# K and Q transposed as pairs of heads in four-byte elements, in a fused kernel of segment-recurrent attention and linear-memory attention

## The chip, the cores and the metric

One Trainium2 chip, one of its cores. The metric is the device time of one execution in microseconds. The engines are TensorE (PE in the profile, its weight loads PEld), VectorE (DVE), ScalarE (ACT), GpSimd (POOL) and SyncE (SP, which issues DMAs).

## What is computed

Two mixers read the same x of 2048 rows by 512, and a gate for each row blends them. A is recurrent: 64 segments of 32 rows, each with 8 memory rows in front that are the first 8 output rows of the segment before. So there are 40 tokens, 32 heads of 128, and each segment's projections can only start when the one before has ended. B is local attention in 4 blocks of 512 rows with 32 heads of 16 and a linear memory; it does not depend on A.

```python
def _A_ref(x, mem0, Wq, Wk, Wv, Wo, seg_len):
    ...
    for s in range(n_seg):                       # 64
        h = concatenate([mem, x[:, s*32:(s+1)*32]], axis=1)      # 40 x 512
        q, k, v = (einsum('btd,dhe->bhte', h, W) for W in (Wq, Wk, Wv))
        scores = where(mask, einsum('bhqe,bhke->bhqk', q, k) * scale, -1e9)
        o = einsum('bhqk,bhke->bhqe', softmax(scores), v)
        o = einsum('bhte,hed->btd', o, Wo)
        mem = o[:, :8]
        outs.append(o[:, 8:])
...
g = sigmoid((x * gate_w).sum(-1, keepdims=True))
return g * A_ref(x, ...) + (1 - g) * B_ref(x, ...)
```

## The kernel before, in words

All weights of A lie in SBUF. A segment is one call of `p_seg` (L1434). Its 40 tokens are split: 24 rows of x and the 8 memory rows (32 tokens, in `hT`) go through the loop; the last 8 rows of x ("the rest") depend on nothing and are projected ahead for four segments at once in `p_rest` (L1364), 16 groups, with V of the rest carried through DRAM.

For each segment and each half r of the heads (16 heads):

- `project` (L1462) calls `wproj` (L1401): 16 matmuls in four column groups of 32, so that the four quadrants of a PSUM bank hold heads by tokens. K, Q and V each come out as 128 by 512. Q of the second half is done in two pieces of 256 columns. `copy` (L998) moves each piece to SBUF as bf16, on ACT (L1002) or DVE (L1002 too; L1000 where DVE is prescribed).
- `ktr` (L1475) transposes the pieces of K and Q on DVE in blocks of 32 by 32 (L1482), from `st` into `KT` (128 by 32 heads by 32 tokens) and `QT` (128 by 32 heads by 40 tokens). 128 transposes of K with 512 elements, 64 of Q with 512, 128 of Q with 256. Q of the rest comes from `rem_q` by a copy on POOL (L1459); it was transposed in `p_rest` (L1398).
- `p_s` (L1486): a matmul writes the mask (H), then 16 matmuls take the scores of one head each (L1497: `KT` of a head stationary, 32 columns; `QT` of a head moving, 40 columns), and 4 take those of the rest's keys for four heads each (L1501: the rest's K stationary, with a step of four elements; 4 by 16 columns of `QT` moving). ACT takes the exponential (L1505).
- `p_u`: sums by a matmul with ones (L1520), their inverse by two ACT operations (L1524, L1526), and products (L1528 on DVE, L1530 on DVE or POOL). Then values (PV L1561, PW L1570), evicted into `OT`, and `wo` (L1290): 64 matmuls (L1310), a transpose of the sum in PSUM (L1328), two small swaps (L1331) and an addition (L1333) that write the next segment's memory rows.

Matmuls of one segment's chain leave TensorE free in places; V's projections, the rest's projections, the output of the rest (`p_orest`) and all of B's work (logits L1142, exponentials L1160 on ACT, masks L1166 on POOL, values L1183, its outputs L1197 to L1245) fill them.

The order of the work on each engine is written out: `ORDER` (L15) is a packed list of operation numbers for each of TensorE, ACT, DVE, POOL and SP, and every engine runs its list in order. `sequences` (L472) unpacks it; `schedule` (L263) replays it to choose PSUM banks, and `waits` (L488) finds the semaphore waits from what each operation reads and writes. An operation that may run on two engines (an eviction: ACT or DVE) runs on the one whose list holds it. The first matmul into a PSUM slot of the pool "F" also waits for what the slot's later operations need, such as a staging buffer `stg` whose output transfer must have left (L270).

The costs given to operations (`cost=`) only served to make the lists; the chip does not see them.

Of the kernel before, what the change touches and what calls it, by code (L numbers as in the profile page):

```python
# [11 lines left out]
F32 = mybir.dt.float32  # L12
# [3 lines left out]
    "c-nPY2S60p)1P;RJ-DNsVj;vXV6WKu+d;8w)EJE#>=<K-1rvLV9UE$FF?K~X=2KD8U`2^FmT1JD7!?aB?S#F3`_0=cTaMg$g}vE%Q-1TCdCwgsjjsc;P5N9f(|hpZr|IU**3HYeK"  # L16
    ">`ry-t^Loz|iHL3)@Ux2yrm(V!g0`!T8${!7FCT^n{@sg|YRb7uZbuGh=>Qxcj147H2>4)7GP%c7A~6vjF}&KIrR&d+9vf9&@BCfZ^bmkQE;X8^`AO<^vBIPtF8%gK|gyNHeUe+8"
    "*G9&xNp(c~Af)axJ+qd0E_$0lx!;r{Pbz7X1bI9=MOorp}za<l7<5N<W7>0QSdUUV2anHSa^I*HGml^tWAyB4dPbQCGF}g^szF)F!s{=riHggRQ*JH@N1DcfgNf(aG&$6*NzqUI4"
    "(sZ*B1+oXCg4`wGDHm7wPeeRB=qRme?VX5fK0)P@H<>;b3|kq=;kb+Jr-eL88B-UMa~+^Vkye>54)4Q^(edC=FoUF{hU$Hu&ov`dde+!wHAEYS=8xfYU#7yOIBzGN!gZOFq7N{U*"
    "zC1H3k$WQ((DM{c2-)s&z1LT+tx@?nS6MVx%YTSKUYlS{=Jp=l{0aUCvGZRcUrdSWn;W`iDj}qfD9MXw>P<+q4U3aSkbS3yOLmu(Thk$G!A;%xUhldx<;kj%@;<xw~e#IL#bFV*z"  # L20
    "ob2+?Lf%=xo)4Dw6PJzjf?cm?q3VUR9OAVPK(mX`f}prB6!=bBVao^a0y8R(*#N^Am6a8Dh0*xF@fNy=QJXv)AfPCZ)7$k+C!rC0Gv)z!IYrxlJvbcTAu$RiGyQMY*<PorPrfw^O"
    "gezet<E%uH2_VU%9_U~LFoOS2Q7l${{yi+E%mz8>(H#Gmoh8bL09WGb8%PMj<WW>`cYrv$8o`E<avLvff;z)t57=>Jq0*Cb>T!<3hBSf@(lq(0q#AKVyzR<c@{if?OWzNFJ=QXqf"
    "a8f^;#4M+v=g!LJ7MK@d`dS!g<U|iTU61xCm?+AS+FPWdIY7-Sv?oXEPac5E?c>4~dC=>;f1pd$^*!EdW1e3PzT08};GdVT1*pl)nwT{*aNedUnF=r9@BoQiV2?ZTYuMDMog24qK"
    "X&*Jt7Zg~Z60f{!*6$@c^DF&}=8TZG|sImI4jQ=weAz?nZ}LWzKfK|VSIu53o9{;UVOD*&yMq9tK0Kr|Cpj9>A=k7GC+ydPodT>$<y;ClTlXldOH9<H20sW@5t-2BU}@_ist&=cQ"
    "WO93kn+oA3RB)^VA582*ZE#Q31v(XL&&zh3h$7(C^F7N>)3ooU;fh=KH!OXJ2aV)uc{ycBs4Tt+;!CkN4SXNm9MpTLetDtAlHGE)c<yZph-4DG3vl9CxK9FTM+<>}R74w}qmkiZ`"
    "y<-ZrPvc<;{CZm=2<dUXZwN+w8{$jwxA9@mg8}~G-eJx8jMyNV`{76|OW5aoCGlPWF;xKCVJ?V~S={*u$K4tQCkeDkMOLx>xoKEiru|eqN&XnVey@J_0K-C;R472jj8u@V_6*^n-"
    "sdnwHhVOpaOVIojIV#LU__90O69PQ3<3r?-v|xUMy<EV(i!+#BXNq8tZM(AT{|P>LDdHq9(_ItvFip&UM75vlGXk$$8PcwINtw*-=_X=DluqemV<#iVeMqJd#z=%jLSvvwq(@@pD"
# [12 lines left out]
    "|HpjH%?t~IQWQwCrO&2@jMJo_GH!v<~hQNJ4+ikCo2JD8J1a&!FH<3z@&4}(&tak(ynpo6$3|esG-@=d;0$(}dH-DavHu$Bh9@k{C2)T=z&d_04<<7`+-UQ}++1G8R-DJ&%hQu9%"  # L40
    "1_AL+X?)1?@hkNfFCA}?M0AOtS$5Iedn9B!V@$yRR~W-$%rfCH`dxs3Ey+M<1b%NyEeBz;UW&lICW21#_WuSllij&F(G9Oz{B+oj@&Yheh5il*LUgK*&RFpUz1C;H!+3ka`tJ~Px"
    "&T_*g?%PCJ8)fAc1T7jabneO3VI2R(N@2NNz&g1)`p1<-qXrNndwV3mPEjL$@=witRe}Wm;^pXheMdJg)<0FozEDLJ8yeY35AZ01fxp`?9W1V)Za*IWS~RHP|R&JbQJV11o1X2fe"
    "M=-RxrA235)9-?b<-#ZdD6-U)Es|qO4?*-YWU^eLUEv{0LZ4RT)>hGy!J@QaR9BrB>jnnUW|nqM-0h8-18gr+ZkCSE81#$J5~dO>Is#4F~Ml8*3h}2sTr_i!Uk#BpzA=Unh(?HxJ"
    "fq$+uh!iB9fTA{WeiAv6rDy9hV|n!%m&&x7^89haAV6DIt_s5Qt~1kZ=kw8lOK=i-mmOf#Q;P^s6u5?idDd};cd9*diCtqC0MY>wMRu~FJ*jIIVc!;Nt8B`|RNy4doRZXDtR!pvF"
    "Lxl?hkZb)xu!R8xm0xwGJ%jWYYz0nuQ`->fqC2cB0O_WkAD!2lXK+6AXFK3bDtdru6)L641lg&l_|EL=ZMqJB^H^Yfu1;;|_;db@&z5VLKo%-YA$qU?wrgqG^&}Gql=E1gRRm(H^"
    ">8r-VQj<ROlUunR*#4?bROtQMl*{oIaLFRhkQ#NunvHuYH~_<ZpHzc+ab{*sjV{aduwvqc{LcvV-3L#*)1oIe3H@&Ey=t-FROSpR5Pht75*thQkp-0Nz5kz}W*4mRR}DS<Fn!))s"
    "Xu*kxQpaQ*lmje2Up?^1vM#oR1E~0(YVPK1L(+=m;J`A!j0)5zvJ0UCoMG++BStnB4+!CPf^4E-mtX%$m(?5`T~wjSRxq=N9RrNI&Gz6R{Ww0crBcYu1sHA<PEr80b+y_hr4i;T0"
    "U4!ya~6iaHpoOCgrX*_+Sp;vEyDf^j`}7@H%Y&Yu`+q{=Dzb-V1&_ccm$eOc`-_QD-2fGhxoJ)IMtov;T5EOjlkR$)})|aV)BHzq0~YbalrDU-*0<)cCW8SAn-6<q(p)&aYk4kU9"
    "s2cYiT?NfSDDJ)tAlqV1TsL7hh8b?d^BA?;71vx4N2F(?<{P2l(yy>H*EOF2p^zJozJ0k#?GDd^2s-P5nfDBP~)dIR3k{1WJgZDo!@7kJ9i**`ENYp#qk9O)4P|FY|`$0_ApSgCz"
    "?{0le?B&hDnw*OQGuWEmyc)1sP(ECZ7{f`YfdVc3t0fr=<S`Tw(9=KgM88S<<V~|Pp{)wwk?NbsE5@WaH=FLbmgVW9-z-rx|+qgp&6BxVhGr?VG%>3ZJ-&Q!(^B_L0TawQ)RR48w"  # L50
    "5wqZbX`goO?i~$qr1R(dDs;<9^@IDh(CFz2Jm&L6r=w{tBsXDCpVdF|I*$3nTZ(EtnY+025rF6?cOh5+RwX;e(r?%DV>jY9h>f!OwQtpQILg*P9hp`49Rtn&KHs$*g|@i@Y=Galu"
# [525 lines left out]
T_TP = 0.72  # L577
# [6 lines left out]
class Kernel:  # L584
# [849 lines left out]
    def p_seg(self, s):  # L1434
# [16 lines left out]
        def by_head(t):  # L1451
            return t.rearrange("p (l q) -> p l q", l=4)
# [179 lines left out]
```

## Time and profile before

| | us |
|---|---|
| three runs | 828.84, 830.23, 834.37 (median 830.23) |
| the profiled execution | 829.86 |
| its span, first to last instruction | 827.8 |
| TensorE busy | 798.0 |
| DVE busy | 680.0 |
| ACT busy | 555.1 |
| POOL busy | 262.0 |
| granted TensorE clock, mean | 0.998 |

In a group of the profile stand line, engine, operation, destination and sources by the program's names, shapes, count, busy microseconds, mean nanoseconds of one, and the engine's idle time in front of them with what ended it. In a row of waits stand who waited, for whom, microseconds in total, times, and the longest. In the chain of waits stand start, length and what. A busy TensorE is not TensorE at its peak, since matmuls overlap.

### The profile page before, as it was taken

The page shows a single profiled execution, that of the slowest core. Times are in us where ns is not written, and L with a number is a line of the kernel's source. Part 1 is how long each engine was busy: PE and PEld are TensorE (multiplying, and loading weights), DVE is VectorE, ACT ScalarE, POOL GpSimd, SP SyncE. Part 2 cuts the span into 40 slices and gives each one's busy share as a digit, 9 for nine tenths or more (in the row PEclk, how much of TensorE's full clock was granted, in tenths as well). Part 3 has the DMA queues.
Part 4 walks back from the last instruction along what each step waited for, and adds up shares of the span by engine and source line. Part 5 has one row for each costly group of instructions (what it writes and reads, how often), then busy time and mean ns, then how long its engine had stood idle before and what let it go on. Part 6 is the DMA issues. An engine that isn't in the chain of part 4 may idle for free.

```text
span 827.8 us, 51780 instructions
## 1 busy us (share of the span) xinstructions
PE 798.0 (96%) x23605; PEld 509.8 (62%) x23613; DVE 680.0 (82%) x1606; ACT 555.1 (67%) x1264; POOL 262.0 (32%) x573
## 2 busy tenths in 40 slices
PE   8899999999999899999998999999999999999987
PEld 4456676657666476666666566565766665656655
DVE  4779778898888689787887998898877788987887
ACT  3667666776667567767666666667667667776763
POOL 3552231333223322431422232323513323323440
PEclk9999999999999999999999999999999999999999
DMA  9973201121200311111011101110111110000001
GB/s 331 411 239 56 52 26 35 34 51 27 53 19 14 52 26 36 34 39 39 15 38 46 38 21 42 18 40 20 40 46 27 26 34 17 15 25 22 22 21 36
DMA packets 71696, 45.14 MB, mean 55 GB/s; under 512 B 50046, under 2 KB 69942, under 8 KB 69942
## 3 DMA queue, kind: packets, MB, share of 16 engines
q1 hardware_dynamic: 70422, 40.92, 17.4%
q8 instruction: 185, 3.03, 1.4%
q10 hardware_dynamic: 1056, 0.92, 0.4%
q14 instruction: 33, 0.27, 0.1%
HBM read 30.33 MB, written 8.87 MB: 47 GB/s over the span
## 4 chain that ended last, share of the span: by engine, by line
PE 80%; DVE 7%; DMA 4%; ACT 3%; issue 2%; POOL 2%; SPq 1%; DVEq 0%; POOLq 0%
PE pb L1412 44%; PE pb L1310 16%; PE pb L1025 6%; PE pb L1142 3%; PE pb L1183 2%; PE pb L1561 2%; PE pb L1497 2%; DMA st<-in_gate_w_dram 2%; PE pb L1520 2%; DMA out_dram<-stg 1%; PE pb L1027 1%; DVE KT_sb L1482 1%; DVE QT_sb L1482 1%; DVE V_sb L1002 1%; PE pb L1570 1%
## 5 line engine op out<-in xcount | busy, mean ns | idle before, releaser
L1002 ACT ACTIVATE st<-pb 128x512 bf16<-128x512 f32 (+2 forms) x294 | 142.3, 506 | 93.8 <-PE pb L1412 73.7
L1160 ACT ACTIVATE PTB<-pb 128x640 bf16<-128x640 f32 x240 | 158.9, 704 | 36.7 <-PE pb L1142 27.9
L1412 PE MATMUL pb<-Wv_sb,hT 128*32 128x512 bf16 x2048 | 154.3, 380 | 0.7 <-issue 0.7
L1412 PE MATMUL pb<-Wq_sb,hT 128*32 128x512 bf16 (+1 forms) x3072 | 139.7, 309 | 0.1
L1412 PE MATMUL pb<-Wk_sb,hT 128*32 128x512 bf16 x2048 | 134.4, 380 | 0.6 <-DVE hT L1333 0.4
L1310 PE MATMUL pb<-Wo_sb,OT_sb 128*32 128x256 bf16 x4096 | 131.9, 273 | 1.1 <-issue 0.5
L1166 POOL TENSOR_SCALAR_AFFINE_SELECT PTB<-PTB 128x512 bf16<-128x512 bf16 x120 | 78.0, 650 | 111.7 <-ACT PTB L1160 105.8
L1310 PEld LDWEIGHTS pb<-Wo_sb,OT_sb 128*32 128x32 bf16 x4096 | 101.5, 96 | 14.5 <-issue 2.0
L1412 PEld LDWEIGHTS pb<-Wq_sb,hT 128*32 128x32 bf16 x3072 | 83.4, 97 | 43.3 <-issue 2.4
L1530 POOL TENSOR_TENSOR PT_sb<-PT_sb,rc_sb 128x64 bf16<-128x64 bf16 x81 | 29.1, 359 | 237.5 <-ACT rc_sb L1526 226.4
L1482 DVE STREAM_TRANSPOSE KT_sb<-st 128x512 bf16<-128x512 bf16 x128 | 89.0, 696 | 12.0 <-ACT st L1002 10.5
L1482 DVE STREAM_TRANSPOSE QT_sb<-st 128x256 bf16<-128x256 bf16 (+1 forms) x192 | 93.8, 507 | 3.4 <-ACT st L1002 1.6
L1412 PEld LDWEIGHTS pb<-Wk_sb,hT 128*32 128x32 bf16 x2048 | 57.2, 97 | 43.2 <-issue 2.7
L1002 ACT ACTIVATE OT_sb<-pb 128x320 bf16<-128x320 f32 (+1 forms) x138 | 56.7, 425 | 36.6 <-PE pb L1570 35.6
L1002 DVE CAST OT_sb<-pb 128x320 bf16<-128x320 f32 (+1 forms) x122 | 57.7, 480 | 20.3 <-PE pb L1570 19.9
L1524 ACT ACTIVATE rc_sb<-pb 128x160 f32<-128x160 f32 x128 | 38.9, 304 | 44.5 <-PE pb L1520 38.4
L1002 DVE CAST V_sb<-pb 128x512 bf16<-128x512 f32 x89 | 60.5, 680 | 7.4 <-PE pb L1412 6.1
L1412 PEld LDWEIGHTS pb<-Wv_sb,hT 128*32 128x32 bf16 x2048 | 50.4, 97 | 19.7 <-issue 0.6
L1328 DVE STREAM_TRANSPOSE pb<-pb 128x256 f32<-128x256 f32 x63 | 29.2, 463 | 36.0 <-PE pb L1310 35.6
L1505 ACT ACTIVATE PT_sb<-pb 128x224 bf16<-128x224 f32 x128 | 45.4, 355 | 11.4 <-PE pb L1501 8.5
L1002 ACT ACTIVATE stg<-pb 128x512 bf16<-128x512 f32 (+1 forms) x70 | 39.9, 572 | 15.0 <-PE pb L1412 12.1
L1528 DVE TENSOR_TENSOR PT_sb<-PT_sb,rc_sb 128x160 bf16<-128x160 bf16 x128 | 44.0, 343 | 5.7 <-ACT rc_sb L1526 4.0
(200 smaller groups left out, 1460.4 us busy)
## 6 DMA issues: line engine op xcount, KB each, us to landing
Wv_sb<-in_A_Wv_dram SPq DMA_DIRECT2D x4, 1024.0 KB, 10.0
Wk_sb<-in_A_Wk_dram SPq DMA_DIRECT2D x4, 1024.0 KB, 20.3
Wq_sb<-in_A_Wq_dram SPq DMA_DIRECT2D x4, 1024.0 KB, 27.4
Wo_sb<-in_A_Wo_dram SPq DMA_DIRECT2D x4, 1024.0 KB, 20.9
rest_v<-stg SPq DMA_DIRECT2D x112, 32.0 KB
rem_v<-rest_v SPq DMA_DIRECT2D x28, 128.0 KB
a_rows<-ao SPq DMA_DIRECT2D x63, 32.0 KB
stg<-a_rows SPq DMA_DIRECT2D x15, 128.0 KB
```

The costliest lines, as they stand in the source:

```text
L1002: self.P.op(("act", "dve"), (lambda a: a.activation(dst, src(), ACT.Copy), lambda d: d.tensor_copy(dst, src())), reads=reads, writes=write ...
L1025: ins = pe.matmul(out[32 * c:32 * c + 32], lhsT[:, 32 * c:32 * c + 32], rhs, start=start, stop=stop, tile_position=(0, 32 * c), **kw)
L1160: P.op("act", (lambda dst=dst, src=src: lambda a: a.activation(dst, src(), ACT.Exp, scale=0.25))(), reads=[pair], writes=["%s%d_%d" % (nam ...
L1166: P.op("gp", (lambda pt=pt, ii=ii: (lambda g: g.affine_select(pt, pt, ([[0, len(ii)]] if len(ii) > 1 else []) + [[1, 128]], ALU.is_ge, 0.0 ...
L1310: ins = pe.matmul(pb[so.b][p0:p0 + 32, 0:256], tok(r, g, l), half(h, d, q), start=(r == 0 and g == 0 and l < 2), stop=(r == 1 and g == 3 a ...
L1328: P.op("dve", lambda d: d.transpose(pb[so.b][:, 256:512], pb[so.b][:, 0:256]), reads=[so], writes=[rt], name="turn%s" % name, cost=0.46, p ...
L1412: ins = pe.matmul(self.pb[sl.b][32 * g:32 * g + 32, 0:hi - lo], x[:, c, 0:32], cols, start=(c == 0), stop=(c == C - 1), tile_position=(0, ...
L1482: op("dve", (lambda dst=dst, src=src: lambda d: d.transpose(dst, src))(), reads=["st%d%s" % (i, tag)], writes=["%sT%d%s" % (kind, r, tag)] ...
L1505: op("act", lambda a: a.activation(PT[:, r, :], pb[rb.b][:, 0:224], ACT.Exp, scale=SCALE), reads=[rb], writes=["PT%d" % r, "PT%dr" % r], n ...
L1524: op("act", lambda a: a.activation(rc[:, r, :], pb[rb.b][:, 0:160], ACT.Ln), reads=[rb], writes=[rr], name="ln%d_%d" % (s, r), cost=t_act( ...
L1528: op("dve", lambda d: d.tensor_tensor(mine[r], mine[r], by_head(rc[:, r, :]), ALU.mult), reads=[rp, rr], writes=[rp], name="nrm%d_%d" % (s ...
L1530: op(("dve", "gp"), tuple((lambda e: e.tensor_tensor(rest[r], rest[r], late(rc[:, r, :]), ALU.mult)) for _ in range(2)), reads=[rp + "r", rr],
```

## The change

Five things:

1. `KT` and `QT` hold pairs of heads: for each pair and token, the two heads' values side by side. Sizes stay.
2. The evictions of K and Q (`project`) and of Q of the rest (`p_rest`) write pairs: `paired` gives a destination that is contiguous and a source that reads, for each token i of a pair b, the two heads 32 columns apart in PSUM.
3. The transposes of K, Q and the rest's Q see the bf16 pairs as one f32: 256 elements in place of 512, 128 in place of 256. K of the rest is evicted and transposed as before.
4. The scores read one head of a pair with a step of two elements, stationary and moving (`l % 2`), and the matmuls of the rest's keys read `QT` in the same way, head by head, so that their columns stay in the old order. POOL's copy of the rest's Q moves the same 256 elements, in pairs.
5. `ORDER` is a new list. SP's part of it is the same; TensorE, ACT, DVE and POOL have other sequences. Of the evictions and other operations that may run on two engines, 66 net leave ACT, DVE gets 75 net, POOL loses 9 net. A few planning costs are changed with it.

The core of the diff (the list left out):

```diff
-        self.KT = t("KT_sb", [128, H, 32])
-        self.QT = t("QT_sb", [128, H, L])
+        self.KT = t("KT_sb", [128, H // 2, 32, 2])
+        self.QT = t("QT_sb", [128, H // 2, L, 2])
...
+    @staticmethod
+    def paired(dst, src):
+        return dst.rearrange("p (b i e) -> p b i e", i=32, e=2), lambda: src().rearrange("p (b e i) -> p b i e", e=2, i=32)
...
-        self.copy(st[:, 0:512], lambda: pb[sl.b][:, 0:512], 512, [sl], [rs], "r%sev%d_%d" % (kind, j, r), prio, dve=not j)
+        to, fro = st[:, 0:512], lambda: pb[sl.b][:, 0:512]
+        if kind == "q":
+            to, fro = self.paired(to, fro)
+        self.copy(to, fro, 512, [sl], [rs], "r%sev%d_%d" % (kind, j, r), prio, dve=not j)
...
-        P.op("dve", lambda d: d.transpose(dst, st[:, :]), reads=[rs],
+        src = st[:, :]
+        if kind == "q":
+            dst, src = dst.bitcast(F32), src.bitcast(F32)
+        P.op("dve", lambda d: d.transpose(dst, src), reads=[rs],
...
-        Kr, Qr = (self.group(k, s // 4).rearrange("p (h k s) -> p s h k", h=H, s=4)[:, s % 4] for k in "kq")
+        Kr = self.group("k", s // 4).rearrange("p (h k s) -> p s h k", h=H, s=4)[:, s % 4]
+        Qr = self.group("q", s // 4).rearrange("p (b k s e) -> p s b k e", b=H // 2, s=4, e=2)[:, s % 4]
...
-        op("gp", lambda g: g.tensor_copy(QT[:, :, SEG:L], Qr), reads=[rQr], writes=["qTr"],
+        op("gp", lambda g: g.tensor_copy(QT[:, :, SEG:L, :], Qr), reads=[rQr], writes=["qTr"],
...
+                fro = (lambda rb=rb, n=hi - lo: lambda: pb[rb.b][:, 0:n])()
+                if kind != "v":
+                    dst, fro = self.paired(dst, fro)
...
-                tag, src, h0, h1 = "" if lo == 0 else "b", self.st[i][:, lo:hi], 16 * r + lo // 32, 16 * r + hi // 32
+                tag, src, b0, b1 = "" if lo == 0 else "b", self.st[i][:, lo:hi].bitcast(F32), 8 * r + lo // 64, 8 * r + hi // 64
                 if kind == "k":
-                    dst = KT[:, h0:h1, :].rearrange("p h t -> p (h t)")
+                    dst = KT[:, b0:b1, :, :].rearrange("p b t e -> p (b t e)").bitcast(F32)
                 else:
-                    dst, src = QT[:, h0:h1, 0:SEG], src.rearrange("p (h t) -> p h t", t=SEG)
+                    dst = QT[:, :, :, :].rearrange("p b t e -> p (b t e)").bitcast(F32).rearrange("p (b t) -> p b t", t=L)[:, b0:b1, 0:SEG]
+                    src = src.rearrange("p (b t) -> p b t", t=SEG)
...
-                        ins = pe.matmul(pb[rb.b][32 * g:32 * g + 32, 56 * l + 16:56 * l + 56], KT[:, 16 * r + 4 * g + l, :], QT[:, 16 * r + 4 * g + l, :],
+                        ins = pe.matmul(pb[rb.b][32 * g:32 * g + 32, 56 * l + 16:56 * l + 56], KT[:, 8 * r + 2 * g + l // 2, :, l % 2], QT[:, 8 * r + 2 * g + l // 2, :, l % 2],
...
-                    ins = pe.matmul(by_head(pb[rb.b][32 * g:32 * g + 32, 0:224])[:, :, 0:16], Kr[:, h0:h0 + 4].rearrange("p h k -> p (h k)"), QT[:, h0:h0 + 4, 24:40],
+                    ins = pe.matmul(by_head(pb[rb.b][32 * g:32 * g + 32, 0:224])[:, :, 0:16].rearrange("p (b e) q -> p b e q", e=2),
+                                    Kr[:, h0:h0 + 4].rearrange("p h k -> p (h k)"), QT[:, b0:b0 + 2, 24:40, :].rearrange("p b t e -> p b e t"),
```

More of the change, by code (lines that the diff above doesn't have):

```diff
@@ L20 @@
[L20 to L27, printed above, removed]
@@ new lines @@
+    "o}-UlLQEyp%Znl@BL;{n;K2$&H>mTz4SFmT->}>Uj3k}Ax1#@|F)jy%a)CuJat}R+mVI0VSn<{jtTiAHr)-JHnVW?7+7^4Mjwxk0EEq7O){4P{F=1({YSvLVSQH!nLG4W_PiTg50"
+    "2~?Cjevt%qpGqX9JTf2%N|n43{DSW=?CJH`$aW^l;(b7AT27at_>WV<G2E+e=NC_xT4})(%_O;1cK|@!%sMuR5FrosV`z$GZL-ngj8W-QHDeyQR&AmT>-AJX~r9w&EP<vf>k13>}"
+    "YuMGWGzU!~8%&JQ-1f(c4LLI~N5IeQV0#?OF2!QE<RZ?L2efGsfP4iSf(uCn}cIN$12`{P+6F9gn+{LDZu1y+Cn%`e0KXaOQp5~=dwr?T)a2rjn0i#RdRP*D_60^lgLUW?-3T5AD"
+    "jybi^^oj}%>U%zo>Jb8OZ<N}L1(=#JDDoS_`pkgh2B0%=U>r|~rbo`cqusO2TW~0a<WCe1=<RUh>xlYGAT@awnt*sMpDAF5er(SIgaCr*VEC!Gp!1GiZ{)5^AJm?7j_+?@1XVC66"
@@ L80 @@
+    "otJL@)wL)-4c5)Eh!1`hDh{$_A@<Vb|sQd)O1)$wQuoV;zaLpB2sUUG%@u)ir8Hvb%k@Q&+V{k_rZ)KoSV_7cgq@(S1DUvNK#LR{$nJCG1bu4xjj1#%~6r$Iq{M$pvdwnLH^THot"
+    "upoOFI4qnez@%WfFs`viutmZQdpIeqVhij8t2925ks5$_xUQH^<o9B@t;c^s`Rkbk6PF+<V06afwJJsk~0Y%s!0(11U#Po^{Crh@eUSOyA{~o~Y!o_aVu1^h;qS`Oa0n|1KhDk~~"
+    "HKvKt?22LT~j&J#_d&CQ;15DVx(()emyhe-)x)ft#V(jKEIrad-db{{MseY1svyrY!5cK-+N&y_s"
 )
@@ L677, in alloc @@
             self.xT[1][:, :, :].rearrange("p c x -> p (c x)")[:, 0:1280], self.OT[:, :, :, :].rearrange("p g h q -> p (g h q)")]
-        self.spread = self.KT[:, 0:16, :].rearrange("p h t -> p (h t)").rearrange("p (l m) -> p l m", l=4)
+        self.spread = self.KT[:, 0:8, :, :].rearrange("p b t e -> p (b t e)").rearrange("p (l m) -> p l m", l=4)
         self.gwr, self.mem0 = self.st[1], self.st[0]
@@ L1327, in wo @@
             turned = lambda: pb[so.b][:, 256:512].rearrange("p (c e t) -> p e c t", c=4, e=2)
-            P.op("dve", lambda d: d.transpose(pb[so.b][:, 256:512], pb[so.b][:, 0:256]), reads=[so], writes=[rt], name="turn%s" % name, cost=0.46, prio=prio)
+            P.op("dve", lambda d: d.transpose(pb[so.b][:, 256:512], pb[so.b][:, 0:256]), reads=[so], writes=[rt], name="turn%s" % name, cost=0.468, prio=prio)
             for e in range(2):
@@ L1331, in wo @@
                 P.op(("act", "dve"), ((lambda a, dst=dst, src=src: a.activation(dst, src(), ACT.Copy)), (lambda d, dst=dst, src=src: d.tensor_copy(dst, src()))),
-                     reads=[so, rt], writes=["other%d" % e], name="swap%s_%d" % (name, e), cost=(0.24, 0.19), prio=prio)
+                     reads=[so, rt], writes=["other%d" % e], name="swap%s_%d" % (name, e), cost=(0.2, 0.195), prio=prio)
             P.op("dve", lambda d: d.tensor_tensor(mem[0], turned()[:, 0, :, 24:32], self.other[:, :, :], ALU.add),
@@ L1397, in p_rest @@
         dst = self.group(kind, j)[:, 512 * r:512 * r + 512]
-        P.op("dve", lambda d: d.transpose(dst, st[:, :]), reads=[rs],
-             writes=["rem%s%d" % (kind, j % 2)], name="r%stp%d_%d" % (kind, j, r), cost=T_TP, prio=prio)
+        src = st[:, :]
+        if kind == "q":
+            dst, src = dst.bitcast(F32), src.bitcast(F32)
+        P.op("dve", lambda d: d.transpose(dst, src), reads=[rs],
+             writes=["rem%s%d" % (kind, j % 2)], name="r%stp%d_%d" % (kind, j, r), cost=0.44 if kind == "q" else T_TP, prio=prio)
     def wproj(self, sl, kind, r, x, reads, name, prio, n, chunks=False, lo=0, hi=512):
@@ L1470, in project @@
                 dst, rd = (Vs[:, r, :], "V%d" % r) if kind == "v" else (self.st[i][:, lo:hi], "st%d%s" % (i, tag))
-                self.copy(dst, (lambda rb=rb, n=hi - lo: lambda: pb[rb.b][:, 0:n])(), hi - lo, [rb], [rd] + (["st%db" % i] if whole and kind != "v" else []),
+                fro = (lambda rb=rb, n=hi - lo: lambda: pb[rb.b][:, 0:n])()
+                if kind != "v":
+                    dst, fro = self.paired(dst, fro)
+                self.copy(dst, fro, hi - lo, [rb], [rd] + (["st%db" % i] if whole and kind != "v" else []),
                           "%sev%d_%d%s" % (kind, s, r, tag), prio)
```

117 lines of the change are left out of this document (59 added, 58 removed).

## The prediction

> **What bounds the kernel now.** I read the page's busy table first, then the stretches (busy time of each engine by window), the waits of TensorE, the chain of waits around the longest hole, and the groups by form for prices.
>
> ```profile
> span 827.8 us, 51780 instructions
> PE 798.0 (96%) x23605; PEld 509.8 (62%) x23613; DVE 680.0 (82%) x1606; ACT 555.1 (67%) x1264; POOL 262.0 (32%) x573
> ...
> 60.00:780.00 720.00, 702.95 (x21407) 457.20 (x21406) 604.68 (x1428) 495.62 (x1134) 220.09 (x467) 1.00 0.14 33
> 270.00:300.00 30.00, 26.66 (x743) 17.34 (x746) 20.64 (x46) 16.69 (x39) 8.36 (x18) 0.94 0.26 45
> 780.00:828.00 48.00, 40.27 (x1240) 25.93 (x1232) 36.86 (x85) 24.84 (x64) 12.60 (x28) 1.00 0.10 29
> ```
>
> In the stretches the first number is the length, the second TensorE's busy time, then PEld, DVE, ACT, POOL, then the granted clock. TensorE is busy for 798.0 of 827.8 us. Between 60 and 780 us it idles 720 - 702.95 = 17.05 us, and 30 - 26.66 = 3.34 us of that lie in one window, where the granted clock also falls to 0.94. Over the last 48 us it idles 7.7 us. The kernel is bound by TensorE's work, and the change removes none of it: all that can be won is what TensorE waits. What it waits for:
>
> ```profile
> PE pb L1412 <- DMA out_dram<-stg: 3.0, 3, 2.4
> PE pb L1142 <- ACT V_sb L1002: 2.2, 4, 0.6
> PE pb L1561 <- DVE PT_sb L1528: 1.4, 3, 1.0
> PE pb L1142 <- ACT stg L1002: 0.9, 2, 0.5
> PE pb L1142 <- DVE V_sb L1002: 0.8, 1, 0.8
> PE pb L1497 <- DVE QT_sb L1482: 0.7, 2, 0.4
> ...
> PEld pb L1497 <- DVE QT_sb L1482: 6.4, 24, 0.6
> PEld pb L1497 <- DVE KT_sb L1482: 1.8, 9, 0.3
> ```
>
> The transposes that the change shortens (L1482) end only 0.7 us of TensorE's idle time by themselves; the weight loads of the scores wait 6.4 + 1.8 = 8.2 us for them in 33 times, mostly while older matmuls still run. The other waits are for evictions and normalisations that stand in the queues of DVE and ACT. The one long hole is a transfer's:
>
> ```profile
> 278.90 0.10 SPq L986
> 279.01 0.04 issue
> 279.05 4.22 DMA out_dram<-stg
> 283.27 0.04 issue
> 283.32 1.89 PE pb L1412 x13
> ```
>
> An output transfer holds a staging buffer for 4.22 us, and TensorE stands behind it.
>
> **The transposes.** A transpose of 512 bf16 becomes one of 256 four-byte elements, one of 256 becomes 128.
>
> ```profile
> L1482 DVE STREAM_TRANSPOSE KT_sb<-st 128x512 bf16<-128x512 bf16 x128 | 89.0, 696 | 12.0 <-ACT st L1002 10.5
> L1482 DVE STREAM_TRANSPOSE QT_sb<-st 128x256 bf16<-128x256 bf16 x128 | 50.1, 412 | 0.7
> L1482 DVE STREAM_TRANSPOSE QT_sb<-st 128x512 bf16<-128x512 bf16 x64 | 44.6, 697 | 2.7 <-ACT st L1002 1.6
> L1328 DVE STREAM_TRANSPOSE pb<-pb 128x256 f32<-128x256 f32 x63 | 29.2, 463 | 36.0 <-PE pb L1310 35.6
> L1219 DVE STREAM_TRANSPOSE t_sb<-pb 128x512 f32<-128x512 f32 x32 | 22.5, 703 | 3.0 <-PE pb L1183 3.0
> L1398 DVE STREAM_TRANSPOSE rem_q<-stg 128x512 bf16<-128x512 bf16 x32 | 22.4, 701 | 1.9 <-ACT stg L1002 0.7 <-POOL QT_sb L1459 0.7
> ...
> L939 DVE STREAM_TRANSPOSE adot<-pb 128x128 f32<-128x128 f32 x4 | 1.2, 296 | 0.0
> ```
>
> 512 f32 take 703 ns and 512 bf16 696 ns: the price goes by elements, not bytes. For 256 four-byte elements in SBUF the bounds are 412 ns (as many bf16) and 463 ns (f32 in PSUM); I take 440. For 128 the bounds are 296 ns (from PSUM) and 412 - (696 - 412)/2 = 270 ns; I take 285. K: 128 x (696 - 440) = 32.8 us; Q whole: 64 x 257 ns = 16.4; Q halves: 128 x 127 ns = 16.3; Q of the rest: 32 x 261 ns = 8.4. DVE sheds 73.9 us (69 to 79 by the bounds). V and the rest's K stay as they are.
>
> **The new order.** SP's queue is the same, entry by entry, so no DMA is moved past another. TensorE runs the same 2979 steps; changes between its tile modes go from 382 to 380, which I cost at nothing. What moves is evictions, from ACT to DVE. Their prices:
>
> ```profile
> L1002 ACT ACTIVATE st<-pb 128x512 bf16<-128x512 f32 x168 | 100.2, 599 | 69.1 <-PE pb L1412 66.7 <-PE pb L1025 1.4
> L1002 ACT ACTIVATE st<-pb 128x256 bf16<-128x256 f32 x103 | 38.4, 384 | 9.0 <-PE pb L1412 7.0 <-DVE ao L1341 1.0 <-PE pb L1025 0.7
> L1331 DVE COPY other_sb<-pb 64x32 f32<-64x32 f32 x99 | 18.7, 189 | 5.0 <-ACT other_sb L1331 1.8
> L1002 DVE COPY st<-pb 64x256 f32<-64x256 f32 x40 | 17.1, 428 | 1.2
> L1002 DVE CAST st<-pb 128x512 bf16<-128x512 f32 x24 | 16.4, 685 | 5.4 <-PE pb L1412 5.3
> L1002 DVE CAST st<-pb 128x256 bf16<-128x256 f32 x25 | 9.9, 397 | 0.1
> ```
>
> Counted in the two orders, DVE takes over 57 evictions of 512 (K 26, Q 16, the rest 12, B's 3; 57 x 685 ns = 39.0 us) and 32 of 256 (12.7 us), and four products each for adot and t1 from POOL (8 at about 0.44 us, 3.5 us); it gives back 17 partial sums (7.3 us) and 6 small swaps (1.1 us). That is +46.8 us, so DVE ends near 680.0 - 73.9 + 46.8 = 653 us. ACT loses 57 x 0.599 + 32 x 0.384 = 46.4 us and gets 17 x 0.38 + 6 x 0.19 = 7.6 back: near 516 us. Neither is the bound, so these sums are not gains; they shorten queues in which TensorE's banks and operands stand.
>
> **The paired eviction** reads PSUM with a step of 32 elements between the two of a pair. No row steps so in PSUM. Lower end: nothing extra. L1331 reads runs of 8 with jumps, 32 elements in 189 ns, and L1002 reads 256 contiguous ones in 428: 1.07 ns an element between them, and contiguous reads of 256 and 512 differ by (685 - 397)/256 = 1.13, so jumps cost nothing there. Upper end: rate halved, that is (599 - 384)/256 = 0.84 ns more an element on ACT, 0.43 us for 512. I take nothing, by the nearer row. [...]
>
> **The scores** (L1497, L1501) read K and Q with a step of two.
>
> ```profile
> L1497 PEld LDWEIGHTS pb<-QT_sb,KT_sb x2048: 92/93/98, 50.4 to 818.5; 128*32 128x32 bf16 x187
> L1497 PE MATMUL pb<-QT_sb,KT_sb x2048: 179/179/193, 50.4 to 818.6; 128*32 128x40 bf16 x187
> L1501 PEld LDWEIGHTS pb<-QT_sb,rem_k x512: 105/107/113, 50.5 to 818.6; 128*32 128x32 bf16 x171
> L1412 PE MATMUL pb<-Wk_sb,hT 128*32 128x512 bf16 x2048 | 134.4, 380 | 0.6 <-DVE hT L1333 0.4
> L1412 PE MATMUL pb<-Wq_sb,hT 128*32 128x256 bf16 x2048 | 75.1, 274 | 0.0
> ```
>
> The one stepped weight load, L1501's with a step of four elements, takes 107 ns where the contiguous one takes 93 (medians). If step two costs the same, 2048 loads are 14 ns longer each, 28.7 us of PEld, which has 828 - 510 us to spare and runs beside matmuls: nothing on the path, and 28.7/4 = 7 us if that cover were gone, as four column groups load side by side. For the moving operand nothing is known. Lower end zero; upper end half rate: a column costs (380 - 274)/256 = 0.41 ns, each pair of heads' groups streams 4 x 40 columns in L1497 and 64 in L1501, 224 x 0.41 = 93 ns, in 128 steps 11.9 us, all on TensorE and so all on the path. I take zero, since even the stepped load at four elements lost only 14 ns over 32 columns, but with little confidence. [...]
>
> **POOL's copy** of the rest's Q (L1459) still moves 256 elements, read in runs of two now instead of single ones:
>
> ```profile
> L1459 POOL COPY QT_sb<-rem_q 128x256 bf16<-128x256 bf16 x64 | 28.1, 439 | 9.0 <-PE pb L1501 2.6 <-DVE rem_q L1398 1.6 <-PE pb L1570 0.4
> ```
>
> I leave it at 439 ns; POOL is idle two thirds of the time, and even 100 ns more would lie beside V's projections.
>
> **The sum.** Waits between 60 and 780 us without the transfer's window: 17.05 - 3.34 = 13.7 us. Bounds are none and all of it; I take half, 6.9 us, because half of what TensorE waits for stands in queues that get shorter and the rest is normalisation, POOL and issue. The last 48 us hold four segments with little other work; each has two transposes in series before its last scores, 257 + 127 ns shorter: 1.5 us. The transfer's hole stays, since SP's order does. The head, where weights arrive, stays. 829.9 us was the profiled execution's own time (span 827.8 and 2.1 around it), 0.4 below the median of 830.2. 829.9 - 8.4 + 0.4 = 821.9, forecast 822 us.
>
> **Rivals.** One: the stepped moving read runs at half rate. 822 + 11.9 = 834 us, within 1%; if nothing is gained either, 842. For it: the stepped weight load; against it: the load's loss is small. Two, the other side: the stepped PSUM read runs at half rate. ACT and DVE would still not be the bound, but each segment evicts five pieces before its scores, and TensorE's order is written for the old price; one eviction of 512 exposed in each segment is 64 x 0.43 = 27.5 us, 849 us. It decides from (838.5 - 822)/64 = 0.26 us exposed a segment on. Against it: L1331. [...] Three: DVE's relief is hidden. TensorE waited only 0.7 us for a transpose itself, and its other waits move elsewhere: 829 us. Four: nearly all waits go, the transfer's hole with them: 829.9 less 17.05 and half of the last 7.7 is 809 us.
>
> **How the numbers follow.** Forecast with reads free and about half the waits gone: 0.42, its own range 814 to 828. Four: 0.10. One: 0.22, of which 0.05 ends over 838.5. Three: 0.11. Two: 0.15. A measurement of this kernel tells about 1% from no change, 821.9 to 838.5 us. Faster: 0.10 + two thirds of 0.42, 0.38. Slower: 0.15 + 0.05 = 0.20. Within: 0.42. The range 810 to 840 leaves out rival two and the ends of one and four.
>
> **What would show it.** Right: transposes at 412 to 463 ns (256 f32) and 270 to 296 ns (128); evictions still at 599 and 685 ns; L1497's matmuls still at 0.18 us; DVE near 653 and ACT near 516 us busy; TensorE's busy time near 798 us and its idle time under 22 us. L1497's matmuls longer by 17 ns (40 columns) and busy time up by 12 us would show rival one; evictions of 512 at 0.8 us or more rival two. What would make the prediction wrong above all is TensorE's busy time itself changing.

## The result, and the profile after

The changed kernel took 824.47 us (median of 8 runs, 823.6 to 828.08) beside 830.87 for the kernel before: ratio 0.9928, interval 0.9904 to 0.9952. Measured again later it took 821.47 us, ratio 0.9880, 0.9858 to 0.9901. A ratio given here can differ by up to 0.0025 from the quotient of the two medians. The forecast was 822.0. So the size came out; which waits would go, and why, did not, as the experiments below show.

The profiled execution took 824.12 us. Its busy table, then its stretches (length, TensorE, PEld, DVE, ACT, POOL, granted clock):

```profile
span 822.2 us, 51771 instructions
PE 795.5 (97%) x23607; PEld 506.2 (62%) x23607; DVE 642.5 (78%) x1681; ACT 523.4 (64%) x1198; POOL 259.7 (32%) x564
```

```profile
60.00:780.00 720.00, 704.37 (x21549) 455.88 (x21545) 571.15 (x1494) 470.03 (x1084) 219.29 (x464) 1.00 0.14 33
270.00:300.00 30.00, 27.82 (x852) 18.99 (x841) 23.06 (x62) 16.52 (x40) 8.82 (x19) 1.00 0.17 39
```

TensorE's steady idle time fell only from 17.05 to 15.63 us, and 1.2 us of that lie in the window from 270 to 300. Its busy time fell by 2.5 us, with the same work. So in this execution idle time is not where most of the gain is seen. But a second execution of the same kernel, of 819.91 us, has a steady idle time of only 720 - 708.05 = 11.95 us:

```profile
60.00:780.00 720.00, 708.05 (x21655) 458.39 (x21658) 575.71 (x1510) 472.76 (x1090) 220.90 (x468) 1.00 0.14 33
```

Waits that the profile puts down to nothing ("issue") make 6.3 us of the idle time in the first execution, 2.8 in the second and 5.4 in before. Single executions of one kernel differ in idle time by more than the change that was to be read from it.

The prices, in groups by form:

```profile
L1002 ACT ACTIVATE st<-pb 128x512 bf16<-128x512 f32 x126 | 75.2, 598 | 71.0 <-PE pb L1422 69.6 <-PE pb L1029 0.5
L1497 DVE STREAM_TRANSPOSE KT_sb<-st 128x256 f32<-128x256 f32 x128 | 54.5, 426 | 7.0 <-ACT st L1002 5.5
L1002 DVE CAST st<-pb 128x512 bf16<-128x512 f32 x66 | 44.5, 674 | 9.6 <-PE pb L1422 8.9
L1497 DVE STREAM_TRANSPOSE QT_sb<-st 128x128 f32<-128x128 f32 x128 | 34.8, 285 | 2.7 <-ACT st L1002 2.0
L1497 DVE STREAM_TRANSPOSE QT_sb<-st 128x256 f32<-128x256 f32 x64 | 27.8, 434 | 5.1 <-ACT st L1002 3.8
L1002 ACT ACTIVATE st<-pb 128x256 bf16<-128x256 f32 x71 | 27.0, 384 | 16.1 <-PE pb L1422 11.1 <-DVE ao L1345 4.1 <-PE pb L1029 0.5
L1002 DVE CAST st<-pb 128x256 bf16<-128x256 f32 x57 | 22.9, 403 | 5.8 <-PE pb L1422 3.9 <-PE pb L1029 1.1
L1470 POOL COPY QT_sb<-rem_q 128x256 bf16<-128x256 bf16 x64 | 29.0, 453 | 43.5 <-PE pb L1516 35.9 <-DVE rem_q L1408 4.0
```

Transposes take 426 to 434 and 285 ns. Paired evictions take what the others took: 598 ns on ACT (599 before), 674 on DVE (685). The scores' reads (minimum, median, maximum in ns; L1512 was L1497, L1516 was L1501):

```profile
L1512 PEld LDWEIGHTS pb<-QT_sb,KT_sb x2048: 92/94/103, 49.3 to 812.5; 128*32 128x32 bf16 x187
L1512 PE MATMUL pb<-QT_sb,KT_sb x2048: 179/181/198, 49.4 to 812.5; 128*32 128x40 bf16 x187
L1516 PEld LDWEIGHTS pb<-QT_sb,rem_k x512: 105/108/116, 49.5 to 812.5; 128*32 128x32 bf16 x171
```

The step of two costs 1 ns in the load and 2 ns in the matmul. And the waits of the scores for the transposes (total us, times, longest), which were 6.4, 1.8 and (for `QT`) 0.7 us before:

```profile
PEld pb L1512 <- DVE QT_sb L1497: 2.4, 9, 0.4
PEld pb L1512 <- DVE KT_sb L1497: 1.7, 6, 0.4
...
PE pb L1512 <- DVE KT_sb L1497: 0.5, 2, 0.3
```

### The profile page after: what moved, and what is told of

It is laid out like the page before. It is cut to its first block, busy times and chain, and to the rows that moved or that the text cites. A ratio compares the mean times of both kernels' runs of the same rounds, so it can differ in the third digit from the quotient of the medians.

```text
span 822.2 us, 51771 instructions
## 1 busy us (share of the span) xinstructions
PE 795.5 (97%) x23607; PEld 506.2 (62%) x23607; DVE 642.5 (78%) x1681; ACT 523.4 (64%) x1198; POOL 259.7 (32%) x564
## 4 chain that ended last, share of the span: by engine, by line
PE 84%; DVE 7%; ACT 3%; DMA 2%; issue 2%; POOL 0%; SPq 0%; DVEq 0%; POOLq 0%
PE pb L1422 45%; PE pb L1314 17%; PE pb L1029 6%; PE pb L1146 4%; PE pb L1577 2%; PE pb L1187 2%; PE pb L1031 2%; PE pb L1512 2%; PE pb L1536 1%; PE pb L790 1%; DMA out_dram<-stg 1%; PE pb L1586 1%; DVE V_sb L1002 1%; PE pb L1235 1%; DVE OT_sb L1002 1%
## 5 line engine op out<-in xcount | busy, mean ns | idle before, releaser
L1002 ACT ACTIVATE st<-pb 128x512 bf16<-128x512 f32 (+2 forms) x232 | 113.1, 499 | 106.8 <-PE pb L1422 80.7
L1422 PE MATMUL pb<-Wq_sb,hT 128*32 128x256 bf16 (+1 forms) x3072 | 140.0, 308 | 0.5 <-DVE hT L1337 0.3
L1422 PE MATMUL pb<-Wk_sb,hT 128*32 128x512 bf16 x2048 | 132.3, 379 | 1.0 <-issue 0.6
L1422 PEld LDWEIGHTS pb<-Wq_sb,hT 128*32 128x32 bf16 x3072 | 80.9, 97 | 41.7 <-DVE hT L1337 3.8
L1422 PEld LDWEIGHTS pb<-Wk_sb,hT 128*32 128x32 bf16 x2048 | 54.6, 97 | 48.9 <-DVE ao L1345 2.2
L1002 DVE CAST st<-pb 128x512 bf16<-128x512 f32 (+1 forms) x123 | 67.2, 549 | 15.4 <-PE pb L1422 12.8
L1002 DVE CAST OT_sb<-pb 128x320 bf16<-128x320 f32 (+2 forms) x121 | 56.5, 475 | 20.6 <-PE pb L1586 18.2
L1497 DVE STREAM_TRANSPOSE QT_sb<-st 128x128 f32<-128x128 f32 (+1 forms) x192 | 61.8, 334 | 7.8 <-ACT st L1002 5.7
L1497 DVE STREAM_TRANSPOSE KT_sb<-st 128x256 f32<-128x256 f32 x128 | 54.5, 426 | 7.0 <-ACT st L1002 5.5
```

Of the source, the lines that this page charges most:

```text
L1002: self.P.op(("act", "dve"), (lambda a: a.activation(dst, src(), ACT.Copy), lambda d: d.tensor_copy(dst, src())), reads=reads, writes=write ...
L1422: ins = pe.matmul(self.pb[sl.b][32 * g:32 * g + 32, 0:hi - lo], x[:, c, 0:32], cols, start=(c == 0), stop=(c == C - 1), tile_position=(0, ...
L1497: op("dve", (lambda dst=dst, src=src: lambda d: d.transpose(dst, src))(), reads=["st%d%s" % (i, tag)], writes=["%sT%d%s" % (kind, r, tag)] ...
```

## The experiments

Two theories stood at the start. One: the shorter transposes take waits off TensorE's path. Two: the gain is the new order's, by accident, above all because the hole at 279 us does not come up. A third came up with the first runs: the layout alone brings the gain, by the time for which VectorE is held, and the new order adds nothing. All ratios are to the kernel before on the same chip.

### Layout and order apart

The changed kernel differs in two things that can be had one by one: the layout (code) and the lists (`ORDER`). For both crossings the planning costs went with the list, so that the order and the PSUM banks are exactly those of the kernel it came from.

```diff
 # the old layout (before) with the new lists
-    "c-nPY2S60p)1P;...
+    "c-nPZ2|yIp8~@(U?...
```

> The new order with the old layout: the lists and the PSUM banks of after, K and Q transposed by 2-byte elements as before (VectorE about 74 us busier than in after, near 716 us). Theory one (the shorter transposes take waits off TensorE): the gain is lost, 830 us or more, since the new list hands VectorE more evictions as well. Theory two (the gain is the new order's, above all that the hole at 279 us does not come up, and VectorE's relief is hidden behind a TensorE that is 97% busy): 824 to 826 us, with PE idle between 60 and 780 us within 1.5 us of after's 15.6 us.

Measured: 869.56 us, ratio 1.0433 (1.0396 to 1.0470). Theory two falls: without the short transposes the new order costs 4%. The waits for the transposes show where:

```profile
PEld pb L1497 <- DVE QT_sb L1482: 24.6, 46, 1.0
...
PEld pb L1497 <- DVE KT_sb L1482: 14.0, 25, 0.9
...
PE pb L1497 <- DVE QT_sb L1482: 11.6, 34, 0.7
PE pb L1497 <- DVE KT_sb L1482: 11.5, 31, 0.8
```

8.9 us of such waits in before are 61.7 us here. The likely reason is that the evictions that the new order gives to VectorE stand in front of the long transposes; no run moves them alone.

```diff
 # the new layout (after) with the old lists
-    "c-nPZ2|yIp8~@(U?...
+    "c-nPY2S60p)1P;...
```

> The new layout with the old order: paired evictions, 4-byte transposes and stepped score reads, every engine's list and the PSUM banks as before. VectorE near 606 us. Theory one: most of the gain is here, 824 to 826 us. Theory two: 829 to 831 us with the hole at 279 us still there. If the stepped reads or the paired evictions cost something that the order hid, it is slower than 831 us.

Measured: 825.99 us, ratio 0.9907 (0.9874 to 0.9939). As far as these intervals tell, the layout alone gives as much as the whole change, with the hole still there:

```profile
PE pb L1422 <- DMA out_dram<-stg: 3.4, 3, 2.4
```

VectorE is busy 616.8 us, where 606 were expected. The scores' waits for transposes are gone altogether; this is all that its waits list for them:

```profile
PEld pb L1512 <- issue: 0.2, 1, 0.2
```

What is late next is ACT: in this kernel VectorE's transposes wait for evictions, 12.1 us in before (10.5 and 1.6) and now

```profile
DVE KT_sb L1497 <- ACT st L1002: 29.1, 63, 1.6
DVE QT_sb L1497 <- ACT st L1002: 12.5, 38, 1.1
```

The recurrence can be read apart from head and tail by the memory additions, 63 instructions whose first and last start stand in the row: before, after, and the old order with the new layout.

```profile
L1333 DVE TENSOR_TENSOR hT<-pb,other_sb x63: 151/191/196, 59.8 to 811.0; 128x32 bf16<-128x32 f32 x63
```

```profile
L1337 DVE TENSOR_TENSOR hT<-pb,other_sb x63: 152/191/193, 57.6 to 804.9; 128x32 bf16<-128x32 f32 x63
```

```profile
L1337 DVE TENSOR_TENSOR hT<-pb,other_sb x63: 153/191/194, 58.4 to 803.0; 128x32 bf16<-128x32 f32 x63
```

751.2, 747.3 and 744.6 us. The 6.6 us between the first and the third are near the 8.9 us of waits that went, but they do not lie where those waits lay. The lists are the same in both, so the 62 stretches between two memory additions can be compared one by one, in one execution of each. TensorE's waits for `QT` and `KT` in before are 9.2 us with those of L1520's loads:

| stretches, by the waits for transposes in before | number | these waits, us | shorter with the new layout by, us |
|---|---|---|---|
| more than 0.3 us | 7 | 3.7 | 2.3 |
| up to 0.3 us | 25 | 5.3 | 1.2 |
| none, around the hole | 1 | 0 | 1.6 |
| none, the others | 28 | 0 | 2.5 |
| the first stretch | 1 | 0.2 | -1.0 |

Single stretches are noisy: between before and the kernel below that only moves one copy on POOL some differ by up to 0.9 us, far from that copy. Still, long waits mostly came back as time and short ones mostly did not. The 1.6 us around the hole can be put down to the clock: the wait there is 2.4 us in both, but over four microseconds behind it the granted clock was 0.69 in before and 1.00 in this execution (the rows stand at the end). The 2.5 us in stretches without such waits must have come to TensorE by other operations behind VectorE, or by chance; this was not taken apart.

### The hole at 279 us

The traces say why it was there in before. POOL (start, length in us) and SP's issues in before:

```profile
273.00 0.73 POOL L1240 TENSOR_TENSOR orow<-adot,t_sb 128x256 bf16<-128x256 f32 x1
273.79 0.26 POOL L1457 COPY hT<-xT 128x96 bf16<-128x96 bf16 x1
```

```profile
274.08 1.22 SPq L910 DMA_TRANSPOSE xT<-in_A_x_dram  x1
275.34 1.89 SPq L1084 DMA_TRANSPOSE stg<-KT  x1
277.28 0.55 SPq L1597 DMA_DIRECT2D a_rows<-ao  x1
277.87 0.45 SPq L986 DMA_DIRECT2D wvB_sb<-in_B_wv_dram  x1
278.36 0.65 SPq L986 DMA_DIRECT2D wqB_sb<-in_B_wq_dram  x1
279.05 0.50 SPq L1287 DMA_DIRECT2D out_dram<-stg  x1
```

and in after:

```profile
267.83 0.26 POOL L1468 COPY hT<-xT 128x96 bf16<-128x96 bf16 x1
```

```profile
268.12 1.23 SPq L910 DMA_TRANSPOSE xT<-in_A_x_dram  x1
...
273.27 0.45 SPq L986 DMA_DIRECT2D wvB_sb<-in_B_wv_dram  x1
273.76 0.50 SPq L986 DMA_DIRECT2D wqB_sb<-in_B_wq_dram  x1
276.81 0.36 SPq L1291 DMA_DIRECT2D out_dram<-stg  x1
```

SP's load of the next x overwrites rows that POOL's copy for segment 19 still has to read. In before that copy stood on POOL behind B's products, so the load left at 274.08, B's weights behind it at 277.87 and 278.36, and the output transfer ran beside them. In after the copy stands ahead of B's products, and the weights have 3 us before the transfer starts. The DMA engines' busy share (the number before the last) from 276 to 280 us, in before and in after:

```profile
276.00:280.00 4.00, 3.49 (x145) 2.31 (x140) 3.15 (x7) 2.40 (x7) 0.80 (x2) 1.00 0.90 85
```

```profile
276.00:280.00 4.00, 3.48 (x132) 2.63 (x128) 2.61 (x7) 2.19 (x5) 0.68 (x2) 1.00 0.12 38
```

One move on POOL, in each direction:

```diff
+        gp = out["gp"]; names = [o.name for o in gp]; hx = gp.pop(names.index("hx19")); names.remove("hx19")
+        gp.insert(names.index("qr18") + 1, hx)          # before: ahead of B's row
+        gp.insert(names.index("bo6") + 1, hx)           # after: behind it
```

> Before, with one POOL instruction moved: the copy of x for segment 19 (L1457) goes ahead of the five operations of B's row that it stood behind. SP's load of the next block of x waits for it, and B's weight loads and the output transfer stand behind that load on SP. If the hole at 279 us comes from this chain (the output transfer of 4.2 us runs beside B's weight loads because these were issued late), it goes, with the half clock behind it: 825 to 827 us, 4 to 5 us less than before. If the transfer is slow for another reason, 830 to 831 us and the hole stays.

Measured: 830.35 us, ratio 0.9967 (0.9940 to 0.9994). The longest wait for an output transfer falls from 2.4 to 1.2 us, and the clock stays at 1.00 there:

```profile
PE pb L1412 <- DMA out_dram<-stg: 1.8, 2, 1.2
```

The chain is as described. Its price is 2.7 us (0.0033 x 832.7), less than expected, with an interval from 0.5 to 5. The 1.2 us are another wait, after 300 us; at 279 us none is left. Between the two memory additions around the hole 14.9 us became 11.3, so on the spot it was worth 3.6 us in these two executions, and part of that was lost elsewhere.

> After, with the same copy moved back behind B's row on POOL, where before has it. If the hole's absence is this one placement, it comes back: 828 to 830 us, with TensorE waiting 2 us or more for the output transfer near 278 us. If the hole went for other reasons (shorter transposes bringing VectorE's blend earlier, for one), the time stays at 824 to 825 us.

Measured: 827.65 us, ratio 0.9915 (0.9884 to 0.9946). The hole is back, with a wait of 2.9 us:

```profile
PE pb L1422 <- DMA out_dram<-stg: 3.3, 2, 2.9
```

The ratio lies between the two that after had (0.9880 and 0.9928), so the time alone decides nothing; that the one placement makes the hole is what the trace shows.

### How long VectorE is held

What else might the layout give? A transpose of four-byte elements can be cut in pieces until it holds VectorE as long as the old one, with layout, reads, evictions, order and banks untouched.

```diff
+def cut(d, dst, src, n):          # n blocks of 32 four-byte elements
+    for lo, hi in ((0, 4), (4, 6), (6, 8)) if n == 8 else ((0, 2), (2, 4)):
+        ins = d.transpose(dst[:, lo:hi], src[:, lo:hi])
+    return ins
```

> The changed kernel itself once more, so that it and the kernels sent with it are measured on one chip: 0.990 to 0.995 of before. Theory three (the layout alone brings the gain, and the new order adds nothing): no less than the old order with the new layout, which had 0.9907. If the new order is worth something of its own, it is 2 us or more below that kernel.

Measured: 821.47 us, 0.9880 (0.9858 to 0.9901), below the expected range and 0.0027, or 2.2 us, below the old order with the new layout. By the letter that speaks for a worth of the order; but the two intervals overlap, and the hole, which only one of these kernels has, accounts for as much.

> After, but each transpose of K and Q cut in pieces: 8 blocks of 32 as 4, 2 and 2, and 4 blocks as 2 and 2, 4-byte elements as in after. From 426 and 285 ns and the slope between them, a piece of 64 elements should take about 214 ns, so the pieces come to 713 and 428 ns together, as long as the 2-byte transposes (696 and 412). Order, layout, reads and evictions stay those of after. If VectorE's time in front of the scores is all that the layout gives, this costs what the old layout cost in the new order: 865 to 875 us. If the layout gave something else as well (reads, evictions), it stays well below, 825 to 850 us.

Measured: 837.41 us, 1.0077 (1.0058 to 1.0097). Slower by 16 us, but far from 869; VectorE's busy time rose by only 30 us, not 74.

> The old order with the new layout and the same cuts: VectorE's transposes last as long as before, all else is the new layout. If paired evictions and stepped reads cost TensorE nothing: 830 to 835 us, 0.997 to 1.007 of before. If they cost something that the shorter transposes paid for, it is slower than before by that: 836 us or more.

Measured: 823.12 us, 0.9901 (0.9877 to 0.9926): no loss at all, which neither expectation had. The dose was too small, as the next runs show. Two instructions of VectorE in a row overlap, as in this stretch of after (start, length):

```profile
271.39 0.45 DVE L1497 STREAM_TRANSPOSE KT_sb<-st 128x256 f32<-128x256 f32 x1
271.76 0.38 DVE L1221 TENSOR_TENSOR t_sb<-t_sb,rmem 128x256 f32<-128x256 f32 x1
```

The second starts 0.37 us after a start of 0.45 us length. By the median of such neighbours a transpose of 512 two-byte elements holds VectorE for 628 ns in before, one of 256 four-byte elements for 359 (K's) to 368 (Q's) in after, the one cut coarsely for 488 (235 + 127 + 126). So the cut was made finer: pieces of 2, 2, 1, 1, 1, 1 and 2, 1, 1 blocks.

> After, with K's and Q's transposes cut finer: 8 blocks as 2, 2, 1, 1, 1, 1 and 4 blocks as 2, 1, 1. In the earlier cut pieces the next instruction started 126 ns after a piece of 64 began and 235 ns after one of 128 (a whole one of 256 holds VectorE for 368 ns, one of 512 two-byte elements for 628), so the earlier cut gave back only 488 of 628 ns. With about 90 ns for a piece of 32 these come to about 614 and 307 ns, against 628 and 327 in before. If the layout's worth is the time that VectorE is held, this is as slow as the new order with the old layout was: ratio 1.035 to 1.05. If something else in the old layout made that kernel slow, it stays at 1.01 to 1.02.

Measured: 873.66 us, 1.0532 (1.0495 to 1.0570), a little above the range. A piece of 32 holds VectorE for 93 ns, so the pieces come to 625 and 312 ns.

> The old order with the new layout and the finer cuts, so that VectorE is held about as long as in before (614 and 307 ns for 628 and 327). If VectorE's time is what counts, and the old order only hides the first part of it (the coarser cut cost nothing there), this has 0.997 to 1.003 of before. If the gain in the old order comes from something other than VectorE's time, it stays at 0.990.

Measured: 829.80 us, 1.0010 (0.9989 to 1.0031). The gain is gone, and the waits of before are back (6.4, 1.8 and 0.7 us there):

```profile
PEld pb L1519 <- DVE QT_sb L86: 6.4, 23, 0.6
...
PEld pb L1519 <- DVE KT_sb L86: 2.6, 11, 0.3
PE pb L1519 <- DVE QT_sb L86: 0.9, 3, 0.5
```

So the time for which the transposes hold VectorE is, within the interval, the whole of what the layout gives, and stepped reads and paired evictions together cost no more than 0.3%. That the pieces are more instructions is not what costs: the coarse cut has 576 more than before had and lost nothing in this order. Last, the fine cut for one kind alone, in the old order:

```diff
-    lambda d: cut(d, dst, src, n)
+    lambda d: cut(d, dst, src, n, kind != "k")    # K's in pieces, Q's whole; and the other way round
```

> The old order with the new layout, only K's transposes cut fine (about 614 ns again), Q's and the rest's Q short. All of them short had 0.9907 and 0.9901 of before, none short 1.001, so 0.0105 is to be divided. In before, weight loads of the scores waited 1.8 us for KT and 6.4 us for QT. By these waits K carries a fifth of the gain: 0.992 to 0.993 here. By the time for which VectorE is held K carries about half: 0.995 to 0.996. If K's transpose, the first of the segment, sets the end, most of it: 0.998 to 1.001.

Measured: 824.68 us, 0.9929 (0.9904 to 0.9954).

> The same with only Q's transposes and the rest's Q cut fine, K's short. By the waits for QT and KT, Q carries four fifths of the gain: 0.998 to 0.999 here. By the time for which VectorE is held, about half: 0.995 to 0.996. If K sets the end, 0.990 to 0.992.

Measured: 823.84 us, 0.9921 (0.9891 to 0.9950). Either half alone gives nearly all of it. No one way of dividing the gain fits both runs: by the waits K's came out and Q's did not. (The 0.9901 that the expectation counts as "all of them short" is the coarsely cut kernel.) The scores' waits do not add either: 2.1 us with K's cut alone, 2.3 with Q's, 9.9 with both.

```profile
PEld pb L1519 <- DVE KT_sb L86: 1.5, 6, 0.3
PEld pb L1519 <- DVE QT_sb L86: 0.6, 3, 0.3
```

```profile
PEld pb L1519 <- DVE QT_sb L86: 2.3, 11, 0.3
```

All of it in one table:

| order | transposes | VectorE busy, us | ratio |
|---|---|---|---|
| old | short | 616.8 | 0.9907 |
| old | cut coarsely | 646.7 | 0.9901 |
| old | K cut finely | 648.6 | 0.9929 |
| old | Q cut finely | 654.2 | 0.9921 |
| old | two-byte (before) | 680.0 | 1 |
| old | cut finely | 684.7 | 1.0010 |
| new | short (after) | 642.2 | 0.9880, 0.9928 |
| new | cut coarsely | 672.1 | 1.0077 |
| new | two-byte | 711.2 | 1.0433 |
| new | cut finely | 716.6 | 1.0532 |

In the old order the time is flat up to some 650 us and has lost about 1% at 680. In the new order every microsecond on VectorE above 642 costs 0.4 to 0.7 us (from after to the coarse cut 30 us of VectorE for 12 to 16 us, to the two-byte row 69 for 42 to 46). The same engine time costs more there, probably because the new order puts more of K's and Q's evictions on VectorE, in front of the transposes; that was not tested by itself. The two last rows differ by 8 us where VectorE differs by 5.4; some 4 to 6 us of that are left without a cause.

### Without the new order

> The old order with the new layout, and the copy of x for segment 19 moved ahead on POOL as in the earlier kernel with only that move. The two gains were 0.0093 and 0.0033 of before, at separate places (the segments' transposes, and the hole at 279 us): if they add, 0.987 of before and about 3 us below after. If the shorter transposes had already taken what the hole costs, 0.990 to 0.992, as with the layout alone.

Measured: 819.35 us, 0.9850 (0.9823 to 0.9877), where after had 0.9880 (0.9858 to 0.9901) on the same chip. The two gains add within their intervals. It is the fastest kernel of the study, but not told apart from after; it shows that the new list is not needed. Like with like, the new list never does better: with the hole in both, 0.9915 with it and 0.9907 without; without the hole, 0.9880 and 0.9850. It takes the hole away, and it brings back 4.6 us of the scores' waits.

## Why the prediction came out, point by point

**What bounds the kernel.** TensorE, right. "All that can be won is what TensorE waits", counted as idle time, was too narrow. In the old order the layout takes 7.3 us off the span; idle time is 2.4 us of that (29.8 to 27.4) and busy time, for the same work, 4.9 (798.0 to 793.1), 1.6 us of which can be the clock behind the hole. The loads' waits "mostly while older matmuls still run" were taken as cover. By the stretches, that holds for most of the short waits and mostly fails for the long ones: about 3.5 us of the 9 show as time where they stood. The rest of the gain came in other places, and how is open.

**Transposes.** 426 to 434 and 285 ns against 440 and 285 taken. By the lengths of its records VectorE shed 72.9 us in the old order (744.1 to 671.2), as the 73.9 say. In busy time, which counts an overlap once, it is 63.2: neighbours overlap by about 77 ns, and 721 pairs do so in place of 859. The "69 to 79 by the bounds" is a slip; the bounds taken give 67 to 82.

**New order.** By lengths VectorE got back 42.0 us (671.2 to 713.2) where 46.8 were counted, and ACT lost 38.4 (612.9 to 574.5) where 38.8 were; in busy time it is 25.7 and 30.2. That these sums are not gains was right: beside the layout and the hole the order is worth nothing that these runs can tell.

**Paired evictions and stepped reads.** Zero, as taken, but for 1 and 2 ns; rivals one and two are out. The load at step two takes 94 ns and at step four 108. Contiguous it took 93, so of the 14 ns that were feared one is there. Evictions of 512 take 598 ns on ACT and 674 on DVE, beside 599 and 685 before. Half rate, for either read, was the author's upper end; no run shows it.

**POOL's copy.** 453 ns for 439. The waits for it are short: 0.7 us in all before, 0.4 after.

**The sum.** 6.9 us of steady waits was a half taken for want of better. Of the 13.7 us that it halves, 13.5 are left in the first execution of after and 9.9 in the second; what went for certain is the hole, which was to stay, and half of the scores' waits, which were taken as covered. The size agrees by luck. The sign "idle time under 22 us" did not come: 26.7 and 23.8 us. Of the 1.5 us in the last four segments little came: from the fourth-last memory addition to the end of the span it is 52.5 us in before, 52.0 and 51.5 in after, and 52.6 in the old order with the new layout. "The transfer's hole stays, since SP's order does" failed: SP's list is the same, but POOL's is not, and SP's load waits for POOL. Only SP's queue was followed there, not what the entries on it wait for.

**Rival three**, relief hidden, falls by the layout alone, which had 0.9907 with every list as before. **Rival four** had the hole right and the size wrong.

## What to carry over

A weight load that waits while older matmuls still run may or may not be lost time (of some 9 us of such waits here about 3.5 showed as time where they stood): sum such waits by what they wait for, beside the idle time, then compare two kernels with the same order stretch by stretch, to see which waits came back as time. Two totals that agree do not show that one is the other. Nor does one execution: read idle time from two. Where a change brings a new order with a new price, cross the two before crediting either, and give back the price in doses, since what an engine's relief is worth depends on what the order has put in front of the waiting work (a microsecond of VectorE above 642 cost 0.4 to 0.7 us in the new order; in the old one up to some 650 cost nothing). And when queues keep their order, follow what each entry waits for on other engines.

## What the runs showed of the hardware

A transpose by VectorE is paid by elements in these runs: four bytes wide 32 cost 170 ns (after with the finer cuts), 128 285 and 256 426 (after), and 512 703 from PSUM (before), where 512 of two bytes cost 696 (before). Neighbours on VectorE overlap by about 77 ns, the median of 859 such pairs in before; in after it is 78, of 925.

In these executions the granted clock fell after some holes and not after others. The four microseconds behind the hole, in before, in after with the late copy, and in the old order with the new layout, whose hole ends three microseconds earlier:

```profile
284.00:288.00 4.00, 4.00 (x65) 1.98 (x60) 1.52 (x3) 0.98 (x2) 0.78 (x2) 0.69 0.05 14
```

```profile
284.00:288.00 4.00, 3.98 (x56) 1.84 (x60) 1.63 (x3) 0.35 (x2) 2.35 (x5) 0.61 0.00 0
```

```profile
280.00:284.00 4.00, 3.69 (x84) 2.26 (x88) 2.04 (x5) 1.63 (x4) 1.47 (x3) 1.00 0.06 16
```

0.69, 0.61 and 1.00, after waits of 2.4, 2.9 and 2.4 us. In before the clock is 0.50 from 284 to 286 us, 0.77 in the next microsecond and 1.00 after it. Two more executions differ in the same way: in the old order with the finer cuts, whose longest wait for an output transfer is 2.0 us, it is 0.94 over 270 to 300 us, as in before; with the coarse cuts, where that wait is 2.5 us, its mean over the whole execution is 1.0, beside 0.998 in before. A fall costs an estimated 1.2 to 1.6 us in these stretches (4 x 0.31, 4 x 0.39), if work goes with the clock. What decides whether the clock falls was not shown.
